# Rectified hidden values by the bank: one rectification per 512 columns instead of two, tiles in pairs, weight roundings in other ticks

## The chip, the cores and the metric

The kernel runs on one core of one Trainium2 chip. The metric is the device time of one execution in microseconds (us), the median of three runs. The engines are named as the profile names them: PE (TensorE, with PEld for its weight loads), DVE (VectorE), ACT (ScalarE), POOL (GpSimd) and SP (SyncE, which issues most DMAs). SBUF is the on-chip memory that all engines reach; PSUM is the memory into which PE writes its products, in banks of 512 fp32 columns.

## What is computed

Attention with global and local keys over 2 x 768 tokens, then a mixture of four experts, then a layer with a softmax-gated unit, a normalisation and an output product. The change touches the experts and, in names alone, the last layer:

```python
x = attention(q, k, v)                      # 1536 x 512
p = domain_probs / domain_probs.sum(-1)
for e in range(4):
    h = np.maximum(x @ w1[e], 0.0)          # 512 -> 1024 hidden values
    out += p[:, e:e + 1] * (h @ w2[e])      # 1024 -> 512
h = out @ w_in;  solu = h * softmax(h)
y = layernorm(solu) * g_ln @ w_out
```

## The kernel before, in words

**Precision.** Every matrix is held as a high part (rounded to PE's fp32r type) and a low part (what the rounding left). A product is three passes on PE: high x high, high weights x low tokens, low weights x high tokens. So for each rectified tile two instructions are needed: ACT writes the high part `fhh` (Relu, which rounds on writing) and DVE writes the low part `fhl`, max(x, 0) minus the high part.

**Order of work.** The experts are cut into eight halves (`he` = 0 to 7) of 512 hidden values. For each half from the second on, the product x @ w1 of tokens 0 to 1023 comes from seven block products instead of eight (`paired_groups`, L639: "paired group" below), once for each of two hidden halves q. From `he` = 2 on the last 512 tokens also come from seven block products (`tail_groups`, L559: "tail group" below), six times in all. The order on PE in one half is: tail group, second product h @ w2 of the last 512 tokens (four output tiles, L524), paired group, second product of tokens 0 to 511, second product of tokens 512 to 1023. The whole program is written out in order by hand (`manual_schedule`): each engine runs its instructions in the order of the code, and waits by semaphores on what it reads or overwrites.

**The tail group** issues the block products in the order 1, 2, 6, 5, 7, 3, 4 (L579), each of 12 matmuls of 256 columns, into three banks: products 1, 6, 7 and 4 into bank a, one after the other, product 2 into b, 5 and 3 into c. ACT copies products 1, 6 and 5 to SBUF (L594). DVE adds (L599): 1 + 2 into b, 5 + 7 into b, 6 + the sum in c into c. Below these are "sum 2", "sum 7" and "sum 3". After each sum, and for product 4 straight from bank a, `hidden` (L571) rectifies the bank's 512 columns in two halves, one for each q:

```python
for q in range(2):
    t = src[:, q_ * q:q_ * q + q_]
    th, tl = (d[2 * q + odd][:, q_ * half:q_ * half + q_] for d in h3)
    nc.scalar.activation(th, t, AF.Relu)                          # L575, ACT
    nc.vector.scalar_tensor_tensor(out=tl, in0=t, ...)            # L576, DVE
```

Hidden tiles 0 and 2 (`odd` = 0) come from products 2 and 3, tiles 1 and 3 (`odd` = 1) from 7 and 4. The first output tile of the second product (`g2`, dt = 0, L524) takes its twelve matmuls in a sorted order: the four high ones of tiles 0 and 2, the four of tiles 1 and 3, then the four low ones.

**The paired group** issues 1, 2, 6, 5, 7, 4, 3, each for q = 0 and then q = 1, with 6 matmuls of 512 columns for each q. There are two banks each of a, b and c. ACT copies products 1, 6 and 7 to SBUF (L673); DVE makes sum 2 in b, sum 7 (the copy of 7 plus bank c) in SBUF over the copy, and sum 3 in c (L677); L654 on ACT and L655 on DVE rectify 512 columns at a time. Product 4 goes to bank a after product 7.

**Weights.** A ring of w2 pieces is loaded by SP (L279, alternately into `kr` and `frawt`), rounded by ACT into `wV` (L295) and completed by POOL (L303). `tick` (L414) starts this: it runs steps that are due, and begins new pieces (`split_steps`, L307) that were loaded at least two ticks ago. `moe` calls `tick` after each group, in the tail group after products 2, 5, 3 and 4 (L781). The same ticks issue the conversion of the last layer's double-precision weights (L186 to L203, most of it on DVE).

**Tiles.** The pool of rectified tiles (L792) has eight buffers of 128 x 512 for each of the tags "hh" and "hl".

## Time and profile before

| | us |
|---|---|
| median of 3 runs (746.58 to 746.95) | 746.9 |
| the profiled execution, whole | 746.98 |
| its span, first to last instruction | 745.2 |
| PE busy | 729.3 |
| DVE, ACT, POOL busy | 476.6, 296.7, 261.4 |

The span is what the trace shows; the profiled execution is 1.8 us longer than its span and 0.1 us longer than the median. A matmul's busy time is modelled and matmuls overlap, so PE's pace is read from start to start, not from the duration of one. In a timeline row the number after "x" is how many like instructions were merged, and a bracket at the end gives the idle time of the engine just before and what ended it.

### The profile page before, as it was taken

The page shows a single profiled execution, that of the slowest core. Times are in us where ns is not written, and L with a number is a line of the kernel's source. Part 1 is how long each engine was busy: PE and PEld are TensorE (multiplying, and loading weights), DVE is VectorE, ACT ScalarE, POOL GpSimd, SP SyncE. Part 2 cuts the span into 40 slices and gives each one's busy share as a digit, 9 for nine tenths or more (in the row PEclk, how much of TensorE's full clock was granted, in tenths as well). Part 3 has the DMA queues.
Part 4 walks back from the last instruction along what each step waited for, and adds up shares of the span by engine and source line. Part 5 has one row for each costly group of instructions (what it writes and reads, how often), then busy time and mean ns, then how long its engine had stood idle before and what let it go on. Part 6 is the DMA issues. An engine that isn't in the chain of part 4 may idle for free.

```text
span 745.2 us, 11046 instructions
## 1 busy us (share of the span) xinstructions
PE 729.3 (98%) x3917; PEld 600.8 (81%) x3917; DVE 476.6 (64%) x1064; ACT 296.7 (40%) x692; POOL 261.4 (35%) x294
## 2 busy tenths in 40 slices
PE   8999999999999999999999999999999999999997
PEld 6687877888887888888788888878888888888886
DVE  6787867647694696668568567765842646655551
ACT  4777766422522333233243424324333323243252
POOL 5600044475783163208306423540644231000000
PEclk9999999999999999999999999999999999999999
DMA  8623421212242132223223222322210820222221
GB/s 248 169 90 108 116 72 44 85 42 72 83 136 79 56 101 70 85 85 114 72 60 96 67 90 85 113 63 66 70 29 29 327 96 9 62 76 75 63 73 48
DMA packets 49985, 65.70 MB, mean 88 GB/s; under 512 B 6656, under 2 KB 31488, under 8 KB 49920
## 3 DMA queue, kind: packets, MB, share of 16 engines
q1 hardware_dynamic: 49360, 64.47, 27.6%
q8 instruction: 33, 0.54, 0.3%
q10 hardware_dynamic: 560, 0.43, 0.2%
q14 instruction: 32, 0.26, 0.1%
HBM read 49.12 MB, written 11.56 MB: 81 GB/s over the span
## 4 chain that ended last, share of the span: by engine, by line
PE 91%; DVE 4%; ACT 4%; issue 1%; DVEq 0%; ACTq 0%
PE fg L524 35%; PE fg L668 18%; PE fo L897 9%; PE fh L836 9%; PE fg L589 6%; PE fg L500 5%; PE x L1095 2%; PE sps L991 2%; PE pt L1073 2%; ACT fhh L575 2%; DVE fg L599 1%; DVE fhl L576 1%; PE wp L132 1%; PE wp L1178 1%; ACT wV L295 1%
## 5 line engine op out<-in xcount | busy, mean ns | idle before, releaser
L524 PE MATMUL fg<-fhh,wV 128*128 128x512 f32 (+1 forms) x800 | 248.2, 387 | 6.6 <-ACT fhh L575 4.4
L524 PEld LDWEIGHTS fg<-fhh,wV 128*128 128x128 f32 x800 | 146.9, 188 | 46.0 <-ACT fhh L575 15.5
L524 PE MATMUL fg<-fhl,wV 128*128 128x512 f32 (+1 forms) x400 | 149.3, 381 | 0.0
L524 PEld LDWEIGHTS fg<-fhl,wV 128*128 128x128 f32 x400 | 75.0, 188 | 14.8 <-DVE fhl L510 0.2
L303 POOL TENSOR_TENSOR wR<-kr,wR 128x512 fp32r<-128x512 f32 (+1 forms) x28 | 29.0, 1060 | 112.0 <-ACT wR L295 112.0
L668 PE MATMUL fg<-xt,fwS 128*128 128x512 f32 x252 | 58.3, 389 | 0.0
L668 PEld LDWEIGHTS fg<-xt,fwS 128*128 128x128 f32 x252 | 47.3, 188 | 9.8
L668 PE MATMUL fg<-xh,wR 128*128 128x512 f32 x168 | 55.0, 394 | 0.0
L532 DVE TENSOR_TENSOR fg<-fg,pb 128x512 f32<-128x512 f32 x60 | 41.5, 692 | 13.4 <-PE fg L524 13.4
L897 PE MATMUL fo<-xt,fth 128*128 128x512 f32 (+1 forms) x156 | 45.4, 375 | 0.0
L537 POOL TENSOR_TENSOR scr<-scr,kr 128x512 f32<-128x512 f32 x24 | 31.0, 1292 | 40.1 <-DVE kr L536 40.1
L1051 ACT ACTIVATE p<-p,mn 128x256 f32<-128x256 f32 x68 | 33.8, 498 | 27.4 <-DVE mn L1046 27.4
L886 POOL TENSOR_SCALAR fva<-fva 128x1 f32<-128x1 f32 x12 | 3.8, 313 | 113.9 <-ACT scr L885 113.9
L533 DVE TENSOR_TENSOR scr<-fg,scr 128x512 f32<-128x512 f32 x60 | 41.5, 692 | 2.0
L655 DVE SCALAR_TENSOR_TENSOR fhl<-fg,fhh 128x512 fp32r<-128x512 f32 x42 | 28.3, 689 | 19.5 <-ACT fhh L654 19.5
L500 PE MATMUL fg<-xh,wR 128*128 128x512 f32 (+1 forms) x128 | 39.5, 373 | 0.0
L654 ACT ACTIVATE fhh<-fg 128x512 fp32r<-128x512 f32 x42 | 24.3, 595 | 38.0 <-DVE fg L677 37.9
L668 PEld LDWEIGHTS fg<-xh,wR 128*128 128x128 f32 x168 | 31.5, 188 | 8.3 <-ACT kr L673 1.9
L673 ACT COPY kr<-fg 128x512 f32<-128x512 f32 x42 | 24.1, 586 | 31.5 <-PE fg L668 31.5
L200 ACT CAST fr<-fcvs 128x256 fp32r<-128x256 f32 x32 | 11.9, 373 | 61.2 <-DVE fcvs L196 50.8
L303 POOL TENSOR_TENSOR fwS<-kr,fwS 128x512 fp32r<-128x512 f32 x28 | 35.7, 1298 | 1.2 <-ACT fwS L295 1.2
L536 DVE TENSOR_TENSOR kr<-fg,pb 128x512 f32<-128x512 f32 x24 | 16.6, 691 | 28.2 <-PE fg L524 24.7
(213 smaller groups left out, 1545.2 us busy)
## 6 DMA issues: line engine op xcount, KB each, us to landing
kr<-in_wall_dram SPq DMA_DIRECT2D x42, 256.0 KB, 2.6
fr<-in_w_dram SPq DMA_DIRECT2D x32, 256.0 KB, 2.7
w_dram<-fr SPq DMA_DIRECT2D x32, 256.0 KB, 2.4
v<-in_vp_dram SPq DMA_DIRECT2D x10, 512.0 KB, 3.5
frawt<-in_wall_dram SPq DMA_DIRECT2D x14, 256.0 KB, 2.7
xt<-w_dram SPq DMA_DIRECT2D x6, 512.0 KB, 10.3
kr<-in_qk_dram SPq DMA_DIRECT2D x22, 128.0 KB, 3.9
out_dram<-scr SPq DMA_DIRECT2D x11, 256.0 KB, 2.2
```

The lines of the kernel that those rows point to most:

```text
L303: e.tensor_tensor(out=w[:, 1], in0=t, in1=w[:, 0].bitcast(F32), op=ALU.subtract)
L500: nc.tensor.matmul(ps[:, :n], lhsT=w[:, a, k], rhs=b[:, k, cols], start=(k == 0 and i == 0), stop=(k == 3 and i == 2))
L524: nc.tensor.matmul(ps[:, :n], lhsT=w[:, a, k], rhs=b[k], start=(i == 0), stop=(i == 11))
L532: nc.vector.tensor_tensor(out=ps[:, :n], in0=ps[:, :n], in1=pb[:, cols], op=ALU.mult)
L533: nc.vector.tensor_tensor(out=a, in0=ps[:, :n], in1=a, op=ALU.add)
L537: nc.gpsimd.tensor_tensor(out=a, in0=a, in1=t, op=ALU.add)
L589: nc.tensor.matmul(ps[:, q_ * q:q_ * q + q_], lhsT=w[:, a, j], rhs=x[b][j], start=(opens and q == j == m == 0), stop=(j == 1 and m == 2), ...
L655: nc.vector.scalar_tensor_tensor(out=tl, in0=src, scalar=0.0, in1=th.bitcast(F32), op0=ALU.max, op1=ALU.subtract)
L668: nc.tensor.matmul(ps, lhsT=w[:, a, j], rhs=x[b][j], start=(i in (1, 2, 5) and j == 0 and m == 0), stop=(j == 1 and m == 2), skip_group_ch ...
L836: nc.tensor.matmul(ps[:, hf], lhsT=a[:, k, cs], rhs=w[:, b], start=(k == 0 and i == 0), stop=(k == 3 and i == 2))
L897: nc.tensor.matmul(ps, lhsT=a[:, fc % 4], rhs=wo[fc][:, b, c0:c0 + n], start=(fc == 0 and i == 0), stop=(fc == 7 and i == 2))
L1051: nc.scalar.activation(p[:, a], p[:, a], AF.Exp, bias=mn[:, a:a + 1], scale=-1.0, accum_out=st_rs[u][:, a, 0:1])
```

## The change

One operation on ACT and one on DVE now rectify a whole bank in the tail group; two tiles of rectified values become the halves of one 128 x 2 x 512 buffer (four of them for each tag), so that a bank's columns for q = 0 and q = 1 lie behind one another and the second product reads its tile as two pieces of 256 columns. In the paired group the copy to SBUF is taken of product 5 instead of 7, and sum 7 is read from bank a and written to bank b. The weight roundings of the tail group are begun only in the tick after product 2, and pieces may be begun one tick after their load there and in the last block of each half.

```diff
--- before.py
+++ after.py
@@ -411,7 +411,7 @@
 
             return [load, nothing, one, both, parts, store]
 
-        def tick(split=True, quiet=False):
+        def tick(split=True, quiet=False, wait=2):
 
             st.now += 1
             for w in st.work:
@@ -424,7 +424,7 @@
                 f()
             if split:
                 for _ in range(2):
-                    w = split_steps(wait=2)
+                    w = split_steps(wait=wait)
                     if w:
                         st.work.append(w)
             load_piece()
@@ -473,12 +473,15 @@
                 yield
             load_pb(0, 0, NT)
 
+        def two_tiles():
+            return [st.hp.tile([128, 2, HALF], F32R, tag=tag, name=f"{arm}{tag}") for tag in ("hh", "hl")]
+
         def gemm_groups(he, blk, last, given=None):
 
 
             c0, n = blk
             cols = slice(c0, c0 + n)
-            hh, hl = [None] * 4, [None] * 4
+            hh, hl, twos = [None] * 4, [None] * 4, []
 
             def g1(ft):
                 if st.pre and he == 0 and c0 == 0:
@@ -501,8 +504,13 @@
                                          start=(k == 0 and i == 0), stop=(k == 3 and i == 2))
                     if k < 3:
                         yield 3 * n / 2.4
-                th = st.hp.tile([128, n], F32R, tag="hh", name=f"{arm}hh")
-                tl = st.hp.tile([128, n], F32R, tag="hl", name=f"{arm}hl")
+                if st.wS is None:
+                    th = st.hp.tile([128, n], F32R, tag="hh", name=f"{arm}hh")
+                    tl = st.hp.tile([128, n], F32R, tag="hl", name=f"{arm}hl")
+                else:
+                    if ft % 2 == 0 or not twos:
+                        twos[:] = two_tiles()
+                    th, tl = (x[:, ft % 2, :n] for x in twos)
                 if ft == 3 and st.wS is None:
                     nc.vector.tensor_scalar(th, ps[:, :n], 0.0, None, op0=ALU.max)
                 else:
@@ -564,17 +572,16 @@
                      for i, k0, cols in ((1, 0, lo), (2, 2, lo), (3, 2, hi), (4, 0, hi))}
             for i, f in ((5, 0), (6, 1), (7, 2)):
                 right[i] = [[st.xt3[f][j][:, b] for j in range(2)] for b in range(2)]
-            for d, tag in zip(h3, ("hh", "hl")):
-                d[:] = [st.hp.tile([128, HALF], F32R, tag=tag, name=f"{arm}{tag}") for _ in range(4)]
+            twos = [two_tiles() for _ in range(2)]
+            for d, w in zip(h3, range(2)):
+                d[:] = [twos[odd][w].rearrange("p h (q c) -> p q h c", q=2)[:, q] for q in range(2) for odd in range(2)]
             banks, kept = {}, {}
 
             def hidden(src, odd, half):
-                for q in range(2):
-                    t = src[:, q_ * q:q_ * q + q_]
-                    th, tl = (d[2 * q + odd][:, q_ * half:q_ * half + q_] for d in h3)
-                    nc.scalar.activation(th, t, AF.Relu)
-                    nc.vector.scalar_tensor_tensor(out=tl, in0=t, scalar=0.0, in1=th.bitcast(F32),
-                                                   op0=ALU.max, op1=ALU.subtract)
+                th, tl = (x[:, half] for x in twos[odd])
+                nc.scalar.activation(th, src, AF.Relu)
+                nc.vector.scalar_tensor_tensor(out=tl, in0=src, scalar=0.0, in1=th.bitcast(F32),
+                                               op0=ALU.max, op1=ALU.subtract)
 
             for i in (1, 2, 6, 5, 7, 3, 4):
                 c = {1: "a", 6: "a", 7: "a", 4: "a", 2: "b", 5: "c", 3: "c"}[i]
@@ -646,11 +653,12 @@
             right = {1: raw_x(0, lo), 2: raw_x(2, lo), 3: raw_x(2, hi), 4: raw_x(0, hi)}
             for i, f in ((5, 0), (6, 1), (7, 2)):
                 right[i] = [[xt[:, f, b, j] for j in range(2)] for b in range(2)]
-            banks, kept = {}, {}
+            banks, kept, twos = {}, {}, []
 
             def hidden(src, dst, ft):
-                th = st.hp.tile([128, HALF], F32R, tag="hh", name=f"{arm}hh")
-                tl = st.hp.tile([128, HALF], F32R, tag="hl", name=f"{arm}hl")
+                if ft < 2:
+                    twos[:] = two_tiles()
+                th, tl = (x[:, ft // 2] for x in twos)
                 nc.scalar.activation(th, src, AF.Relu)
                 nc.vector.scalar_tensor_tensor(out=tl, in0=src, scalar=0.0, in1=th.bitcast(F32),
                                                op0=ALU.max, op1=ALU.subtract)
@@ -668,13 +676,12 @@
                         nc.tensor.matmul(ps, lhsT=w[:, a, j], rhs=x[b][j],
                                          start=(i in (1, 2, 5) and j == 0 and m == 0), stop=(j == 1 and m == 2),
                                          skip_group_check=(i not in (1, 2, 5)))
-                if i in (1, 6, 7):
+                if i in (1, 6, 5):
                     kept[q, i] = sc_b[(2 if i == 6 else 0) + q]
                     nc.scalar.copy(kept[q, i], ps)
                 if i in (2, 7, 3):
-                    s, u = kept[q, {2: 1, 7: 7, 3: 6}[i]], banks[q, "b" if i == 2 else "c"]
-                    t = s if i == 7 else u
-                    nc.vector.tensor_tensor(out=t, in0=s, in1=u, op=ALU.add)
+                    t = banks[q, "c" if i == 3 else "b"]
+                    nc.vector.tensor_tensor(out=t, in0=kept[q, {2: 1, 7: 5, 3: 6}[i]], in1=ps, op=ALU.add)
                     hidden(t, *((h1, 2 * q) if i == 2 else (h2, 2 * q + 1) if i == 7 else (h2, 2 * q)))
                 elif i == 4:
                     hidden(ps, h1, 2 * q + 1)
@@ -753,7 +760,7 @@
                 for cost in g:
                     yield 0, cost
                 st.tick(st.wS is not None, quiet=(he == 0 and gi < 4) or (given is None and gi in (1, 2))
-                        or (last and gi == 3))
+                        or (last and gi == 3), wait=1 if last and he else 2)
             if he % 2 and he < NHE - 1:
                 st.later.append((st.now + 2, he // 2 + 1, blk))
 
@@ -778,7 +785,7 @@
                 for i in st.tail_groups(he, h3):
                     yield 0, 0.0
                     if i in (2, 5, 3, 4):
-                        st.tick(quiet=True)
+                        st.tick(i == 2, True, 1)
                 yield from run(he, (2 * HALF, 512), False, h3)
             h1, h2 = ([[None] * 4, [None] * 4] for _ in range(2))
             for i in st.paired_groups(he, h1, h2):
@@ -789,7 +796,7 @@
 
     def rest_of_moe(st, arm, gen):
         with ExitStack() as es:
-            st.hp = hp = es.enter_context(tc.tile_pool(name=f"{arm}h", bufs=8))
+            st.hp = hp = es.enter_context(tc.tile_pool(name=f"{arm}h", bufs=4))
             st.wS = es.enter_context(tc.tile_pool(name=f"{arm}wS", bufs=1)).tile([128, 4, 2, 512], F32R, name=f"{arm}wS")
             st.cvp = es.enter_context(tc.tile_pool(name=f"{arm}cvp", bufs=2))
             st.rawt = es.enter_context(tc.tile_pool(name=f"{arm}rawt", bufs=1)).tile([128, 512], F32, name=f"{arm}rawt")
@@ -863,9 +870,9 @@
             def tr(t):
                 tt = t_b[t % 2]
                 res = []
+                twos = [hp.tile([128, 2, HALF], F32R, tag=tag, name=f"{arm}t") for tag in ("hh", "hl")]
                 for g in range(2):
-                    th = hp.tile([128, 512], F32R, tag="hh", name=f"{arm}th")
-                    tl = hp.tile([128, 512], F32R, tag="hl", name=f"{arm}tl")
+                    th, tl = (x[:, g] for x in twos)
                     if 1 < t < NSLOT - 2:
 
                         pt = tq_b[t % 2].rearrange("p (i g c q) -> p g i c q", i=4, g=2, c=4)[:, g]
```

The order of instructions on PE, SP and POOL is the same as before but for names and lines. On ACT and DVE it changes in the tail and paired groups. ACT in the first tail group, before (`fg_2569` is bank a, `fg_2583` b, `fg_2614` c):

```order
L575 ACTIVATE fhh_2561<-fg_2583 128x256
L575 ACTIVATE fhh_2563<-fg_2583 128x256
L594 COPY kr_78<-fg_2569 128x512
L594 COPY kr_78<-fg_2614 128x512
L295 CAST wV_67<-kr_78 128x512
L575 ACTIVATE fhh_2562<-fg_2583 128x256
L575 ACTIVATE fhh_2564<-fg_2583 128x256
L575 ACTIVATE fhh_2561<-fg_2614 128x256
L575 ACTIVATE fhh_2563<-fg_2614 128x256
L295 CAST wV_67<-frawt_1826 128x512
L575 ACTIVATE fhh_2562<-fg_2569 128x256
L575 ACTIVATE fhh_2564<-fg_2569 128x256
```

and now (a, b and c are `fg_2549`, `fg_2563`, `fg_2594`):

```order
L582 ACTIVATE fhh_2545<-fg_2563 128x512
L295 CAST wV_67<-kr_78 128x512
L601 COPY kr_78<-fg_2549 128x512
L601 COPY kr_78<-fg_2594 128x512
L295 CAST wV_67<-frawt_1826 128x512
L582 ACTIVATE fhh_2547<-fg_2563 128x512
L582 ACTIVATE fhh_2545<-fg_2594 128x512
L582 ACTIVATE fhh_2547<-fg_2549 128x512
```

Four rectifications stand where eight stood. The rounding from `kr` has moved from behind the copy of product 5 to ahead of the copy of product 6, and the rounding from `frawt` from between the rectifications of products 3 and 4 to ahead of that of product 7.

The end of the second paired group on ACT, before (`fg_2762` and `fg_2770` are the a banks):

```order
L673 COPY kr_78<-fg_2762 128x512
L654 ACTIVATE fhh_2850<-kr_78 128x512
L673 COPY kr_78<-fg_2770 128x512
L654 ACTIVATE fhh_2862<-kr_78 128x512
L654 ACTIVATE fhh_2872<-fg_2762 128x512
L654 ACTIVATE fhh_2882<-fg_2770 128x512
```

and now (`fg_2734` and `fg_2742` are the a banks, `fg_2793` and `fg_2801` the c banks, `fg_2751` and `fg_2763` the b banks):

```order
L681 COPY kr_78<-fg_2793 128x512
L681 COPY kr_78<-fg_2801 128x512
L200 CAST fr64_2713<-fcvs_1830 128x256
L662 ACTIVATE fhh_2821<-fg_2751 128x512
L662 ACTIVATE fhh_2821<-fg_2763 128x512
L662 ACTIVATE fhh_2840<-fg_2734 128x512
L662 ACTIVATE fhh_2840<-fg_2742 128x512
```

The two copies of bank a between the rectifications are gone; two copies of the c banks stand ahead of them. The same place on DVE, before:

```order
L677 TENSOR_TENSOR kr_78<-kr_78,fg_2823 128x512
L655 SCALAR_TENSOR_TENSOR fhl_2851<-kr_78,fhh_2850 128x512
L677 TENSOR_TENSOR kr_78<-kr_78,fg_2830 128x512
L655 SCALAR_TENSOR_TENSOR fhl_2863<-kr_78,fhh_2862 128x512
L655 SCALAR_TENSOR_TENSOR fhl_2873<-fg_2762,fhh_2872 128x512
L655 SCALAR_TENSOR_TENSOR fhl_2883<-fg_2770,fhh_2882 128x512
```

and now:

```order
L684 TENSOR_TENSOR fg_2751<-kr_78,fg_2734 128x512
L663 SCALAR_TENSOR_TENSOR fhl_2822<-fg_2751,fhh_2821 128x512
L684 TENSOR_TENSOR fg_2763<-kr_78,fg_2742 128x512
L663 SCALAR_TENSOR_TENSOR fhl_2822<-fg_2763,fhh_2821 128x512
L663 SCALAR_TENSOR_TENSOR fhl_2841<-fg_2734,fhh_2840 128x512
L663 SCALAR_TENSOR_TENSOR fhl_2841<-fg_2742,fhh_2840 128x512
```

The two sums now read the a banks themselves and write the b banks, in the same order with the low parts: the second sum still stands behind the first low part.

## Rows read from the trace of the kernel before

**Rows 1.** The page, parts 1 and 4: busy time by engine; the chain that ended last
```profile
PE 729.3 (98%) x3917; PEld 600.8 (81%) x3917; DVE 476.6 (64%) x1064; ACT 296.7 (40%) x692; POOL 261.4 (35%) x294
...
PE 91%; DVE 4%; ACT 4%; issue 1%; DVEq 0%; ACTq 0%
```

**Rows 2.** Waits by engine and line, PE: us in total, times, longest us
```profile
PE fg L524 <- ACT fhh L575: 4.4, 6, 0.7
```

**Rows 3.** The chain in order of time, 220 to 420 us: start us, us, what
```profile
220.59 7.25 PE fg L589 x60
...
227.91 0.71 DVE fg L599
...
230.28 0.70 DVE fg L599
...
231.00 0.39 ACT fhh L575
...
232.26 0.51 ACT wV L295
...
263.01 21.76 PE fg L524 x96
...
356.25 0.71 DVE fg L599
```

**Rows 4.** Timeline of the first tail group, 218 to 236 us: start us, us, engine line op
```profile
226.43 0.59 ACT L594 COPY kr<-fg 128x512 f32<-128x512 f32 x1 [0.37 <-PE fg L589]
...
230.42 0.28 PE L589 MATMUL fg<-xh,wR 128*128 128x256 f32 x1
...
231.44 3.27 PE L524 MATMUL fg<-fhh,wV 128*128 128x512 f32 x8 [0.74 <-ACT fhh L575]
...
235.47 0.39 PE L524 MATMUL fg<-fhh,wV 128*128 128x512 f32 x1
```

**Rows 5.** Timeline of the second paired group, all engines, 247 to 261 us
```profile
247.98 0.70 DVE L677 TENSOR_TENSOR fg<-kr,fg 128x512 f32<-128x512 f32 x1 [1.26 <-PE fg L668]
...
248.71 0.60 ACT L654 ACTIVATE fhh<-fg 128x512 fp32r<-128x512 f32 x1 [1.47 <-DVE fg L677]
...
249.34 0.69 DVE L655 SCALAR_TENSOR_TENSOR fhl<-fg,fhh 128x512 fp32r<-128x512 f32 x1 [0.66 <-ACT fhh L654]
249.95 0.69 DVE L677 TENSOR_TENSOR fg<-kr,fg 128x512 f32<-128x512 f32 x1
...
256.13 0.59 ACT L673 COPY kr<-fg 128x512 f32<-128x512 f32 x1 [0.58 <-PE fg L668]
...
258.01 0.57 ACT L673 COPY kr<-fg 128x512 f32<-128x512 f32 x1
...
258.63 0.19 PEld L668 LDWEIGHTS fg<-xh,wR 128*128 128x128 f32 x1 [0.30 <-ACT kr L673]
```

**Rows 6.** Line L668's instructions: what its engine waited for (us, times)
```profile
  ACT kr L673: 1.9, 7
```

**Rows 7.** Line L655's instructions: durations ns min/median/max, first and last start
```profile
L655 DVE SCALAR_TENSOR_TENSOR fhl<-fg,fhh x42: 678/692/694, 185.4 to 585.9; 128x512 fp32r<-128x512 f32 x42
L655 DVE SCALAR_TENSOR_TENSOR fhl<-kr,fhh x14: 691/693/1117, 194.0 to 580.8; 128x512 fp32r<-128x512 f32 x14
```

**Rows 8.** Timeline of SP's queue, 200 to 560 us: the loads of L279
```profile
221.51 0.33 SPq L279 DMA_DIRECT2D frawt<-in_wall_dram  x1
...
350.85 0.33 SPq L279 DMA_DIRECT2D frawt<-in_wall_dram  x1
```

**Rows 9.** Line L279's instructions: their DMAs' time to landing
```profile
DMA to landing us min/median/max: 2.5/2.7/3.3
```

**Rows 10.** Timeline of another paired group, 447 to 449.6 us
```profile
447.11 0.42 DVE L198 TENSOR_TENSOR fr<-fr,fcvs 128x256 f32<-128x256 f32 x1
...
448.52 0.59 ACT L673 COPY kr<-fg 128x512 f32<-128x512 f32 x1
```

**Rows 11.** The page, part 6: DMA issues, KB each, us to landing
```profile
xt<-w_dram SPq DMA_DIRECT2D x6, 512.0 KB, 10.3
```

## The prediction

> **What bounds the kernel now.** The page comes first: PE is busy for 729.3 of 745.2 us, and the chain that ended last runs over PE for 91% and over DVE and ACT for 4% each [rows 1]. So PE sets the time wherever it has something to do, and a change that leaves its matmuls as they are can gain only where the chain leaves PE. The waits of PE name one such place in the expert stage: six waits on line L575, the rectification in the tail group [rows 2]. The chain in order of time shows what stands there. At 227.91 us it leaves PE for sum 7 on DVE, and then runs through rectifications, low parts, sum 3 and a weight rounding, ACT and DVE in turn, until PE takes over [rows 3]. It does so once in each of the six tail groups.
>
> The timeline of the first tail group shows what the place costs [rows 4]. The last matmul of product 4 starts at 230.42, and such matmuls follow each other at 7.25 / 60 = 0.12 us [rows 3], so PE could go on at 230.54. The second product starts at 231.44, its first eight matmuls are spread over 3.27 us where they need some 1.8, and the next output tile starts at 235.47. Twelve matmuls at the undisturbed pace of 21.76 / 96 = 0.2267 us [rows 3] take 2.72 us. So 235.47 - 230.54 - 2.72 = 2.21 us are lost in a tail group, 13.3 us in six: that is the ceiling of what the change can gain there.
>
> The paired groups hold the other wait, a small one: PE waits seven times, 1.9 us in all, for the ACT copy of product 7, since product 4 goes into the same bank [rows 6]; in the trace the weight load at 258.63 is the one that was held [rows 5].
>
> **Tail group: one rectification for a bank, and the rounding out of its way.** The durations of whole-bank operations, and what one leaves between itself and the next, are taken from the same work in the paired group, where 512 columns are handled at a time already [rows 5]: from the start of a sum to the start of its rectification 248.71 - 247.98 = 0.73 us, from there to the low part 0.63, from a low part to the next sum on DVE 0.61; a rectification takes 0.60.
>
> Sum 7 starts at 227.91 as before, since PE's order ahead of it is unchanged. Then its rectification starts at 228.64, its low part at 229.27, and sum 3 at 229.88 (before: 230.28 [rows 3]); product 3 is long done (its last matmul is 12 x 0.12 us ahead of that of product 4, at 228.98). The rectification of sum 3 starts at 230.61 and ends at 231.21. Before, the first half of it started at 231.00 and ended at 231.39 [rows 3], and PE followed 0.05 us later [rows 4]; so PE starts at 231.26, only 0.18 us earlier. What changes is what follows. The rectification of product 4 no longer has the rounding of 0.51 us ahead of it [rows 3] nor a low part between its halves: it starts behind that of sum 3, at 231.21 at the latest, ends at 231.81, and PE wants it four matmuls on, at 231.26 + 0.91 = 232.17. The low part of 3 starts at 231.24, that of 4 at 231.85, and the latter ends at 232.54; PE wants the low ones after eight matmuls, at 233.07. So none of the twelve is late any more, and the next output tile starts at 231.26 + 2.72 = 233.98 instead of 235.47: 1.49 us in a tail group, **8.9 us in six**. Of the 2.21 us lost, 0.72 stay: the start, which the chain sum 7, rectify, low part, sum 3, rectify still sets. That chain is what is late next.
>
> The two roundings that move: the one from `kr` now stands ahead of the copy of product 6, which frees bank a for product 7; but ahead of both there is now one rectification of 0.60 us instead of two of 0.39 with a low part between them, and the difference covers the rounding's 0.51, so I cost it at nothing. The one from `frawt` fills the time in which ACT waits for sum 7; its load was issued at 221.51 [rows 8] and lands 2.7 us later [rows 9], at 224.2, while ACT reaches it after the copy of product 5, at 226.43 + 0.59 = 227.02 [rows 4]: 2.8 us of cover. POOL's low parts and the next loads follow earlier than before.
>
> **Paired group: sum 7 reads the bank.** Before, ACT's copy freed the second bank a at 258.01 + 0.57 = 258.58, and PE's load followed at 258.63 [rows 5]. Now DVE frees it, with its second sum 7, which stands on DVE behind the first sum, the first rectification (ACT) and the first low part. The first sum can start when the first copy did, at 256.13; then 0.73 + 0.63 + 0.61 us to the second sum and 0.69 us for it, which is 258.79, and PE at 258.84. That is 0.21 us later, in each of seven paired groups: **1.5 us lost**. Its bounds are nil (if the 0.05 us of slack and the shorter read of PSUM make it up) and one operation of DVE more, as below. The copies of product 5 that replace those of 7 run while PE still has both products 7 to do. What waits behind the longer wait: all of PE, in order; rectifications and low parts of the group are not due until the second product, over 2 us later.
>
> The low part now reads a bank where it read SBUF: the rows show 692 ns from a bank and 693 from SBUF [rows 7], so this costs nothing. The Trainium skill (VectorE: DVE Perf Modes, the section on the TRN2 errata) gives a DVE instruction 58 fixed cycles from SBUF and 120 from PSUM, which at its 0.96 GHz would make each low part 0.065 us longer and the seven groups 0.5 us dearer, an estimate from that page. This trace does not agree with it, and the sum goes by the rows.
>
> **Reading tiles in two pieces.** The second product of the tail group now reads its tiles as two pieces of 256 columns. The trace has no such read at full width. From below it costs nothing; from above, each of the 288 matmuls (12 x 4 output tiles x 6) costs what two matmuls of 256 columns do, 2 x 0.1208 instead of 0.2267 us [rows 3], 4.3 us in all. I take nothing, because the columns streamed are the same in number and the extra in that row is per instruction, of which there is still one.
>
> The pairing of tiles itself removes no work and adds no wait that I can place: a buffer's former values were read before the tail group began. The last layer has the same order and sizes.
>
> **Sum.** 8.9 - 1.5 = 7.4 us off the profiled execution's 746.98 us: 739.6; the median stands 0.1 lower, so **739.5 us**. The saving reaches the end, because PE has no other wait in the expert stage that could take it back.
>
> **Rivals.** *Two pieces are slow:* the pace of PE's second product in the tail falls as bounded above, 739.5 + 4.3 = 743.8. Against it: nothing in the rows shows a matmul that pays by piece; for it: nothing excludes it. 7%.
>
> *DVE is not free for sum 7.* Before, the copy on ACT shielded PE from DVE; now a conversion operation (0.42 us) that DVE still has ahead of the first sum 7 holds PE. In the tightest group the last one ends at 447.53, and PE's signal comes at 448.52, 0.99 us later [rows 10]. If the conversions slip so that one operation too many stands there in each group, 7 x 0.42 = 2.9 us are lost, 742.4; 5%. With three, 8.8 us are lost and the change comes to nothing, 748.3 at worst; together with the case that two tiles in a buffer make ACT wait for the other half's readers and nothing is gained at all (746.9), 5%.
>
> *The moved rounding blocks ACT (slower).* In the tail group ACT now takes the rounding from `frawt` before the rectification of sum 7. If the load has not landed, everything behind it waits: rectifications 7, 3 and 4, and PE with them. ACT is due at sum 7 at 228.64 and the rounding holds it 0.51 us, so a load that lands after 228.13, 6.6 us after its issue, delays the chain one for one, and beyond 6.6 + 1.5 = 8.1 us the tail group is slower than before. At 10.3 us, which 512 KB loads take elsewhere [rows 11], it is 3.7 - 1.5 = 2.2 us worse, six times, and with the paired groups 746.9 + 13.2 + 1.5 = 761.6. Against it: these loads landed in 3.3 us at most [rows 9], and the one issued latest in its tail group, at 350.85 [rows 8] for a sum 7 at 356.25 [rows 3], 1.0 us later in it than the first, keeps 1.2 us of cover even then. 4%.
>
> **How the numbers follow.** The forecast as worked out has 79%. The range goes from 737.5 (nothing lost in the paired groups, and 0.5 us more gained by waits too small for the sum) to 743.8 (two pieces at their upper bound), which takes in one conversion in the way. A measurement of this kernel can tell about 0.2%, 1.5 us, from no change: faster by more than that are the forecast and the first two rivals, 79 + 7 + 5 = 91%; within it 5%; slower 4%.
>
> **What would show it.** Right: PE's waits on the tail rectification shrink to one short one per tail group, the next output tile starts 6.1 us after sum 7 instead of 7.6, no rounding stands between rectifications, and PE's held weight load in the paired group grows by some 0.2 us and names DVE. Wrong: ACT waiting for a DMA in the tail group, second-product matmuls there more than 0.23 us apart with no wait, or conversions on DVE between product 7 and its sum.

## The result: 6.6 us faster, in the tail groups

The changed kernel takes 740.1 us (median of 4 runs, 739.95 to 740.36); the kernel before took 746.7 beside it (746.57 to 746.95). The ratio is 0.9911, with an interval of 0.9894 to 0.9929. The forecast was 739.5. The profiled execution took 740.11 us, with a span of 738.2 where it was 745.2.

The page of the changed kernel, parts 1 and 4 (before: [rows 1]):

```profile
PE 725.0 (98%) x3917; PEld 601.8 (82%) x3917; DVE 473.0 (64%) x1040; ACT 293.2 (40%) x668; POOL 260.7 (35%) x294
...
PE 85%; DVE 5%; ACT 4%; issue 3%; POOL 2%; DMA 0%; DVEq 0%; ACTq 0%; POOLq 0%
```

PE has the same 3917 instructions; DVE and ACT have 24 fewer each, which are the 24 second halves of six tail groups. The chain's shares are of little use here: ahead of the tail groups, from some 158 to 194 us, it now runs over POOL and a piece of 10.16 us of "issue" where it ran over PE before, though PE is busy throughout in both. The waits tell more. First the waits of PE's weight loads before, then those after (us in total, times, longest us):

```profile
PEld fg L524 <- ACT fhh L575: 15.5, 24, 0.9
...
PEld fg L668 <- ACT kr L673: 1.9, 7, 0.3
```

```profile
PEld fg L532 <- ACT fhh L582: 4.5, 6, 0.8
PEld fg L676 <- DVE fg L684: 3.6, 7, 0.5
```

Four waits in each tail group have become one, and in the paired groups DVE holds PE for longer than ACT did. The first tail group after (start us, us, engine line op; the rows to compare are [rows 4]):

```profile
227.81 0.70 DVE L606 TENSOR_TENSOR fg<-kr,fg 128x512 f32<-128x512 f32 x1 [2.23 <-PE fg L596]
229.17 0.69 DVE L583 SCALAR_TENSOR_TENSOR fhl<-fg,fhh 128x512 fp32r<-128x512 f32 x1 [0.66 <-ACT fhh L582]
229.78 0.69 DVE L606 TENSOR_TENSOR fg<-kr,fg 128x512 f32<-128x512 f32 x1
...
230.50 1.09 ACT L582 ACTIVATE fhh<-fg 128x512 fp32r<-128x512 f32 x2 [1.36 <-DVE fg L606]
231.12 1.29 DVE L583 SCALAR_TENSOR_TENSOR fhl<-fg,fhh 128x512 fp32r<-128x512 f32 x2 [0.66 <-ACT fhh L582]
...
231.15 2.14 PE L532 MATMUL fg<-fhh,wV 128*128 128x512 f32 x8 [0.56 <-ACT fhh L582]
...
234.04 0.39 PE L532 MATMUL fg<-fhh,wV 128*128 128x512 f32 x1
```

From sum 7 to the next output tile it is 234.04 - 227.81 = 6.23 us; it was 235.47 - 227.91 = 7.56 [rows 3, 4]. Six times 1.33 us are 8.0; in the other five groups it is 6.21 to 6.23 us, and was 7.55 to 7.56. The second paired group, DVE and the load it holds (compare [rows 5]):

```profile
254.71 0.70 DVE L684 TENSOR_TENSOR fg<-kr,fg 128x512 f32<-128x512 f32 x1 [1.05 <-PE fg L676]
256.07 0.69 DVE L663 SCALAR_TENSOR_TENSOR fhl<-fg,fhh 128x512 fp32r<-128x512 f32 x1 [0.66 <-ACT fhh L662]
256.68 0.69 DVE L684 TENSOR_TENSOR fg<-kr,fg 128x512 f32<-128x512 f32 x1
...
257.42 0.19 PEld L676 LDWEIGHTS fg<-xh,wR 128*128 128x128 f32 x1 [0.52 <-DVE fg L684]
...
257.75 0.39 PE L676 MATMUL fg<-xl,wR 128*128 128x512 f32 x1
```

The load is held for 0.52 us instead of 0.30. Seven times 0.22 is 1.5 us, so 8.0 - 1.5 = 6.5 of the 6.6 us are placed.

### The profile page after: what moved, and what is told of

Its sections match the earlier page's. It is cut to its first block, busy times and chain, and to the rows that moved or that the text cites. A ratio compares the mean times of both kernels' runs of the same rounds, so it can differ in the third digit from the quotient of the medians.

```text
span 738.2 us, 11012 instructions
## 1 busy us (share of the span) xinstructions
PE 725.0 (98%) x3917; PEld 601.8 (82%) x3917; DVE 473.0 (64%) x1040; ACT 293.2 (40%) x668; POOL 260.7 (35%) x294
## 4 chain that ended last, share of the span: by engine, by line
PE 85%; DVE 5%; ACT 4%; issue 3%; POOL 2%; DMA 0%; DVEq 0%; ACTq 0%; POOLq 0%
PE fg L532 35%; PE fg L676 14%; PE fo L904 9%; PE fh L843 9%; PE fg L596 6%; PE fg L503 4%; PE x L1102 2%; PE sps L998 2%; PE pt L1080 2%; DVE fg L684 1%; DVE fg L606 1%; ACT fhh L582 1%; PE wp L1185 1%; ACT fhh L662 1%; DVE fhl L663 1%
## 5 line engine op out<-in xcount | busy, mean ns | idle before, releaser
L532 PE MATMUL fg<-fhh,wV 128*128 128x512 f32 (+1 forms) x800 | 243.5, 384 | 3.4 <-ACT fhh L582 3.3
L663 DVE SCALAR_TENSOR_TENSOR fhl<-fg,fhh 128x512 fp32r<-128x512 f32 x56 | 38.1, 690 | 31.8 <-ACT fhh L662 31.8
L662 ACT ACTIVATE fhh<-fg 128x512 fp32r<-128x512 f32 x56 | 32.7, 598 | 58.9 <-DVE fg L684 55.1
L904 PE MATMUL fo<-xt,ft 128*128 128x512 f32 (+1 forms) x234 | 51.8, 374 | 0.0
L904 PEld LDWEIGHTS fo<-xt,ft 128*128 128x128 f32 x234 | 41.5, 188 | 7.6
L684 DVE TENSOR_TENSOR fg<-kr,fg 128x512 f32<-128x512 f32 x42 | 28.9, 689 | 21.6 <-PE fg L676 18.8
```

The source lines that it names most:

```text
L532: nc.tensor.matmul(ps[:, :n], lhsT=w[:, a, k], rhs=b[k], start=(i == 0), stop=(i == 11))
L662: nc.scalar.activation(th, src, AF.Relu)
L663: nc.vector.scalar_tensor_tensor(out=tl, in0=src, scalar=0.0, in1=th.bitcast(F32), op0=ALU.max, op1=ALU.subtract)
L684: nc.vector.tensor_tensor(out=t, in0=kept[q, {2: 1, 7: 5, 3: 6}[i]], in1=ps, op=ALU.add)
L904: nc.tensor.matmul(ps, lhsT=a[:, fc % 4], rhs=wo[fc][:, b, c0:c0 + n], start=(fc == 0 and i == 0), stop=(fc == 7 and i == 2))
```

## Experiments

Ten kernels. Each edit is made in the changed kernel, but for one that is made in the kernel before. "Changed" is 740.11 us throughout; the kernel before took 746.55 to 746.75 beside the various runs.

### The paired group's copy of 7 again

```diff
-                if i in (1, 6, 5):
+                if i in (1, 6, 7):
...
-                    t = banks[q, "c" if i == 3 else "b"]
-                    nc.vector.tensor_tensor(out=t, in0=kept[q, {2: 1, 7: 5, 3: 6}[i]], in1=ps, op=ALU.add)
+                    s, u = kept[q, {2: 1, 7: 7, 3: 6}[i]], banks[q, "b" if i == 2 else "c"]
+                    t = s if i == 7 else u
+                    nc.vector.tensor_tensor(out=t, in0=s, in1=u, op=ALU.add)
```

> The changed kernel with the paired group's old order: product 7 is copied by ACT and sum 7 lies over the copy; everything else as in the change. Theory (the wait for DVE's second sum 7 costs PE 0.21 us in each of seven paired groups): 740.1 - 7 x 0.21 = 738.6 us, PE's held weight load is released by ACT again and its seven waits fall from 3.6 us to about 1.9. Rival A (the longer hold is made up elsewhere, so the paired change costs nothing): 740.1. Rival B (sums and low parts out of PSUM are worth more than the hold, so the old order is dearer): 741 or more.

Measured: 738.72 us (738.43 to 738.81), 1.39 below the changed kernel, as the theory said. The waits of its weight loads:

```profile
PEld fg L532 <- ACT fhh L582: 4.5, 6, 0.8
...
PEld fg L676 <- ACT kr L681: 1.9, 7, 0.3
```

The tail's row is that of the changed kernel, and the paired group's is that of before. So this part of the change costs 1.4 us, for the reason given.

### The old ticks

```diff
-                        st.tick(i == 2, True, 1)
+                        st.tick(quiet=True)
...
-                        or (last and gi == 3), wait=1 if last and he else 2)
+                        or (last and gi == 3))
```

> The changed kernel with the ticks of before: the rounding from frawt stands between the rectifications of products 3 and 4 again; whole-bank rectifications stay. Theory (most of the gain comes from whole banks, the rounding's place matters by what the rectification of 4 is then late): the rectification of 3 starts at 230.50, the rounding 0.50 later, that of 4 ends near 232.1, PE's fifth weight load would be due near 231.95, so 0.15 to 0.25 us in each of six tail groups: 741.0 to 741.6 us. Rival (the gain is the rounding's move): 0.5 us or more in each, 743 to 747. Rival (no one waits for it): 740.1.

Measured: 740.66 us (740.38 to 740.85), 0.55 above the changed kernel. That is less than the theory's 0.9 to 1.5, and it excludes the rival by which the roundings' move is the gain. The rows of the first tail group show a second hold, before the fifth load:

```profile
230.93 0.76 PEld L532 LDWEIGHTS fg<-fhh,wV 128*128 128x128 f32 x4 [0.76 <-ACT fhh L582]
231.94 0.76 PEld L532 LDWEIGHTS fg<-fhh,wV 128*128 128x128 f32 x4 [0.25 <-ACT fhh L582]
```

Its idle time is 0.25 us, but the next output tile comes only 0.05 us later than in the changed kernel: from sum 3 (229.56) it starts after 4.31 us (233.87) where the changed kernel has 4.26. Six times 0.05 is 0.3; the other 0.25 of the 0.55 is placed nowhere, and is less than the spread of either kernel's runs.

### Halves again, roundings moved

```diff
-                th, tl = (x[:, half] for x in twos[odd])
-                nc.scalar.activation(th, src, AF.Relu)
-                nc.vector.scalar_tensor_tensor(out=tl, in0=src, scalar=0.0, in1=th.bitcast(F32),
-                                               op0=ALU.max, op1=ALU.subtract)
+                for q in range(2):
+                    t = src[:, q_ * q:q_ * q + q_]
+                    th, tl = (x[:, half, q_ * q:q_ * q + q_] for x in twos[odd])
+                    nc.scalar.activation(th, t, AF.Relu)
+                    nc.vector.scalar_tensor_tensor(out=tl, in0=t, scalar=0.0, in1=th.bitcast(F32),
+                                                   op0=ALU.max, op1=ALU.subtract)
```

> The changed kernel with the tail group's rectification in two halves of 256 columns again, into the same paired buffers; the roundings stay moved. Theory (whole banks bring most): the rows of before with the rounding's 0.40 taken out give 7.56 - 0.40 = 7.16 us from sum 7 to the next output tile, where the changed kernel has 6.23, so 0.93 in each of six: 740.1 + 5.6 = 745.7 us. Rival (the roundings' move brings most): 741 to 742. This run and the one with the old ticks together tell whether the two gains add: if they do, what they lose sums to about 6 x 1.33 = 8.0.

Measured: 749.15 us (748.76 to 749.55), ratio to before 1.0036 (1.0023 to 1.0048): slower than the kernel before, and 3.4 us above what I expected. The expected 0.93 us in the second product is there (228.19 to 235.28, 7.09 us for 7.16). What I had not seen stands earlier in the group, on ACT and then on PE:

```profile
224.09 0.38 ACT L584 ACTIVATE fhh<-fg 128x256 fp32r<-128x256 f32 x1 [1.63 <-DVE fg L608]
224.97 0.38 ACT L584 ACTIVATE fhh<-fg 128x256 fp32r<-128x256 f32 x1 [0.49 <-DVE fhl L585]
225.25 0.61 ACT L295 CAST wV<-kr 128x512 fp32r<-128x512 f32 x1
225.76 1.08 ACT L603 COPY kr<-fg 128x512 f32<-128x512 f32 x2
...
226.40 1.69 PE L598 MATMUL fg<-wR,fwS 128*128 128x256 f32 x12 [0.30 <-ACT kr L603]
```

The second half waits 0.49 us for DVE, the rounding from `kr` stands behind it, the copy of product 6 behind that, and PE waits for this copy in each of six groups. Sum 7 starts 228.19 - 220.19 = 8.00 us after the group's first matmul instead of 227.81 - 220.36 = 7.45. So a tail group is 0.55 + 0.86 = 1.41 us longer than with whole banks, 8.5 in six; measured are 9.0. Of the rest, 0.35 stands in the fourth group, where sum 7 starts 8.35 us after the first matmul. The prediction cost the rounding ahead of the copy at nothing because one rectification stands before it instead of two with a low part between them; this run shows the bill where that cover is missing.

### Halves and the old ticks

Both edits above at once.

> The changed kernel with rectification in halves and the ticks of before, both at once: what is left of the change is the paired tiles and the paired group's copy of 5. Theory (the pairs cost nothing, the paired group costs 1.4): 746.55 + 1.4 = 748.0 us. With the halves and the moved roundings the time was 749.15, so the move by itself then costs 1.1 us where banks are rectified in halves, though it gains 0.5 where they are rectified whole; the trace of that run shows the reason that this would confirm: PE waited 6 x 0.3 us for the copy of product 6, which stands behind the rounding from kr. With the old ticks that wait is absent. Rival (halves written into paired tiles cost something by themselves): 749 or more, with or without the old ticks. Rival (the two gains add): 749.15 + 0.55 = 749.7.

Measured: 748.90 us (748.73 to 750.81; two of the five executions took 750.8, the profiled one among them). That lies between theory (748.0) and rival (749 or more), and it does not say that the roundings' move costs 1.1 us in this form: 748.90 against 749.15 is nothing that I would call a difference. PE's wait for the copy of 6 is absent, as expected, but the rounding is back between the rectifications, and the two about balance. Of the 0.9 us over the theory, 0.40 are an idle time before sum 7 in the fourth tail group, which the chain calls "issue" (at 421.64 here; the run with moved roundings has it too, so the faster executions of this kernel may as well, which no trace shows). The rest stays open, and with it the rival that halves cost something in paired tiles by themselves; the next two runs speak against it, for halves in another order.

### The same halves, both rectifications first

```diff
+                qs = [slice(q_ * q, q_ * q + q_) for q in range(2)]
                 th, tl = (x[:, half] for x in twos[odd])
-                nc.scalar.activation(th, src, AF.Relu)
-                nc.vector.scalar_tensor_tensor(out=tl, in0=src, scalar=0.0, in1=th.bitcast(F32),
-                                               op0=ALU.max, op1=ALU.subtract)
+                for q in qs:
+                    nc.scalar.activation(th[:, q], src[:, q], AF.Relu)
+                for q in qs:
+                    nc.vector.scalar_tensor_tensor(out=tl[:, q], in0=src[:, q], scalar=0.0, in1=th[:, q].bitcast(F32),
+                                                   op0=ALU.max, op1=ALU.subtract)
```

> The changed kernel with halves of 256 columns again, as in the run at 749.15, but in another order: ACT takes both halves of a bank, then DVE both low parts. The instructions are the same in number and size as in that run. Theory (halves are dear because ACT and DVE take turns on one bank, each half waiting 0.49 us for the other engine, and hardly because there are two instructions): two rectifications back to back take 0.66 us where one of 512 columns takes 0.60, two low parts 0.76 where one takes 0.69, sum 3 comes 0.1 us later than with whole banks: 740 to 741.5 us. Rival (it is the number of instructions): 747 to 749.

Measured: 739.38 us (739.14 to 739.39): 9.8 us below the same instructions in turns, and 0.7 below the changed kernel. Its first tail group:

```profile
228.25 0.66 ACT L584 ACTIVATE fhh<-fg 128x256 fp32r<-128x256 f32 x2 [1.07 <-DVE fg L609]
...
228.94 0.76 DVE L586 SCALAR_TENSOR_TENSOR fhl<-fg,fhh 128x256 fp32r<-128x256 f32 x2 [0.72 <-ACT fhh L584]
229.61 0.69 DVE L609 TENSOR_TENSOR fg<-kr,fg 128x512 f32<-128x512 f32 x1
...
230.33 1.21 ACT L584 ACTIVATE fhh<-fg 128x256 fp32r<-128x256 f32 x4 [1.42 <-DVE fg L609]
...
230.77 2.12 PE L532 MATMUL fg<-fhh,wV 128*128 128x512 f32 x8 [0.47 <-ACT fhh L584]
```

Two halves back to back take ACT 0.66 us where one whole bank takes 0.60. PE starts 230.77 - 230.33 = 0.44 us after the last sum's first rectification, where it was 0.65 with whole banks: its first load needs the first half only. It is the turns that were dear, and not the number of instructions.

### The kernel before with this order alone

The edit is in the tail group's `hidden` of the kernel before, and is its only one:

```diff
-                for q in range(2):
-                    t = src[:, q_ * q:q_ * q + q_]
-                    th, tl = (d[2 * q + odd][:, q_ * half:q_ * half + q_] for d in h3)
+                ops = [[src[:, q_ * q:q_ * q + q_]] + [d[2 * q + odd][:, q_ * half:q_ * half + q_] for d in h3]
+                       for q in range(2)]
+                for t, th, tl in ops:
                     nc.scalar.activation(th, t, AF.Relu)
+                for t, th, tl in ops:
                     nc.vector.scalar_tensor_tensor(out=tl, in0=t, scalar=0.0, in1=th.bitcast(F32),
                                                    op0=ALU.max, op1=ALU.subtract)
```

> The kernel before with nothing changed but this order in the tail group: both rectifications of a bank, then both low parts. No paired tiles, the old ticks, the copy of 7. Theory (the change's gain is the end of the turns between ACT and DVE on one bank, and the paired tiles only the way to it): the changed kernel's 740.1, less 1.4 for the paired group's copy of 5, more 0.55 for the rounding's old place and up to 0.7 for the halves: 739.2 to 740.0 us. Rival (whole banks in one buffer are needed): 745 to 746.7.

Measured: 738.61 us (738.3 to 738.9), ratio to before 0.9891 (0.9875 to 0.9908). The theory's mechanism was right; the time is 0.6 below its range. ACT's two halves now follow each other at once, in the first tail group for sum 7 and sum 3:

```profile
228.29 0.66 ACT L575 ACTIVATE fhh<-fg 128x256 fp32r<-128x256 f32 x2 [1.07 <-DVE fg L600]
230.37 0.66 ACT L575 ACTIVATE fhh<-fg 128x256 fp32r<-128x256 f32 x2 [1.43 <-DVE fg L600]
```

Two lines in another order gain 8.1 us, more than the whole change. Paired tiles and whole banks were one way to end the turns, and not the better one. This kernel and the one before it both rectify in ordered halves, in separate and in paired tiles; they differ by 0.77 us, where the copy of 5 and the roundings account for 1.39 - 0.55 = 0.84. So in this order pairing the tiles costs nothing that the runs can show.

### Sum 3 ahead of the low part of 7

In the tail group `hidden` puts its low part on a list; the list is emptied after every sum or rectification but that of product 7.

```diff
-                nc.vector.scalar_tensor_tensor(out=tl, in0=src, scalar=0.0, in1=th.bitcast(F32),
-                                               op0=ALU.max, op1=ALU.subtract)
+                lows.append(lambda: nc.vector.scalar_tensor_tensor(
+                    out=tl, in0=src, scalar=0.0, in1=th.bitcast(F32), op0=ALU.max, op1=ALU.subtract))
...
+                while lows and i != 7:
+                    lows.pop(0)()
```

> The changed kernel with one DVE instruction moved in the tail group: the low part of product 7 stands behind sum 3 instead of ahead of it. Theory (the chain sum 7, rectify, low part, sum 3, rectify sets the second product's start): sum 3 then starts when product 3 is done, some 0.38 us behind its last matmul, at 229.25 instead of 229.78, PE starts near 230.62 instead of 231.15, and six tail groups gain 6 x 0.53 = 3.2: 736.9 us. If PE's hold also no longer empties its weight loads, some 0.1 more in each, 736.3. Rival (ACT's rectification of 4 or the later low parts then hold PE, so the gain is given back): 739 to 740. Rival (product 3 is the bound already): 740.1.

Measured: 737.18 us (737.05 to 737.42), 2.9 below the changed kernel for 3.2 expected. PE's load is held for 0.25 us instead of 0.76, and the next output tile starts 5.68 us after sum 7 (228.00 to 233.68) instead of 6.23:

```profile
229.45 0.70 DVE L608 TENSOR_TENSOR fg<-kr,fg 128x512 f32<-128x512 f32 x1 [0.76 <-PE fg L598]
230.06 2.08 DVE L585 SCALAR_TENSOR_TENSOR fhl<-fg,fhh 128x512 fp32r<-128x512 f32 x3
...
230.83 1.68 PEld L532 LDWEIGHTS fg<-fhh,wV 128*128 128x128 f32 x8 [0.25 <-ACT fhh L584]
```

Sum 3 now waits for PE, not for DVE's low part. This confirms what the prediction left standing as "the start, which the chain still sets".

### The second sum 7 ahead of the first low part

The same list in the paired group, kept over the first of the two sums 7:

```diff
+                while lows and (i, q) != (7, 0):
+                    lows.pop(0)()
```

> The changed kernel with one DVE instruction moved in the paired group: the second sum 7 stands ahead of the first low part of product 7 instead of behind it; the copies stay those of product 5. Theory (the hold of bank a comes from the low part that stands ahead of the second sum): the second sum starts when PE has finished product 7, near 256.07 instead of 256.68, and ends 0.61 earlier than PE's load wants it or nearly so; the whole delay of the matmul behind the held load, 257.75 - (255.80 + 7 x 0.227) = 0.36 us, goes, in seven groups 2.5: 740.1 - 2.5 = 737.6 us, below the 738.7 of the copy of 7. If only the 0.21 is won back: 738.6. Rival (the wait is for the bank's own readout, so the order on DVE changes nothing): 740.1. Rival (first low parts come late for the second product of tokens 0 to 511): 740 or more.

Measured: 737.12 us (736.95 to 737.48), 3.0 below the changed kernel where 2.5 were worked out (the other 0.5 stays open), and 1.6 below the copy of 7. The second sum starts at 256.08 (256.68 in the changed kernel), the waits of PE's loads have no row for this place any more, and the load that was held follows the one before it after 0.22 us (257.18 to 257.40). So reading the bank was not a bad idea; the order on DVE was what made it cost something.

### Both orders, and both with halves

The two edits together:

> The changed kernel with both DVE orders: sum 3 ahead of the low part of 7 in the tail group, and the second sum 7 ahead of the first low part in the paired group. Theory (two holds that do not touch each other): the tail order gained 740.1 - 737.2 = 2.9, the paired order is expected to gain 1.5 to 2.5, together 734.7 to 735.8 us. Rival (they share DVE's time, so one gives part of the other back): 736.5 or more.

Measured: 734.16 us (734.1 to 734.29). The gains add, as the theory said: 2.93 + 2.99 = 5.92, measured 5.95. To this kernel, one edit more in the tail's `hidden`:

```diff
-                nc.scalar.activation(th, src, AF.Relu)
+                for q in (slice(0, q_), slice(q_, 2 * q_)):
+                    nc.scalar.activation(th[:, q], src[:, q], AF.Relu)
```

> The kernel at 734.16 (both DVE orders) with the tail group's rectification on ACT in two halves back to back, and one low part of 512 columns on DVE behind both. Theory (PE's first loads of the second product need only the first half of the last sum's bank, which is rectified some 0.2 us earlier): PE's hold, 0.25 us in the trace of that kernel, falls to about 0.05 in each of six tail groups, and no rectification gets in the way, since two halves take 0.66 us where one takes 0.60: 734.2 - 6 x 0.2 = 733.0 us. Rival (the hold is not the bound any more, since product 3 or the rectification of product 4 is late next): 733.7 to 734.2. Rival (one instruction more on ACT delays the rectification of product 4, which PE wants 0.9 us after the first): 734.5 or more.

Measured: 732.81 us (732.64 to 733.31), ratio to before 0.9817 (0.9804 to 0.9831). The theory holds: no weight load waits for a rectification in the tail any more. From its page and its first tail group:

```profile
PE 96%; DVE 2%; ACT 1%; DMA 0%; issue 0%; DVEq 0%; ACTq 0%
```

```profile
227.32 0.70 DVE L609 TENSOR_TENSOR fg<-kr,fg 128x512 f32<-128x512 f32 x1 [2.16 <-PE fg L599]
...
229.94 1.69 PEld L532 LDWEIGHTS fg<-fhh,wV 128*128 128x128 f32 x8
...
232.82 0.39 PE L532 MATMUL fg<-fhh,wV 128*128 128x512 f32 x1
```

The next output tile starts 5.50 us after sum 7. PE's last matmul of product 4 starts at 229.83 and the second product at 229.95, 0.12 us on, so PE's matmuls keep their pace there. The load starts only 0.01 us ahead of its matmul, though, and by the prediction's own working 232.82 - 229.95 - 2.72 = 0.15 us of the 2.21 are still lost. This is the fastest version found: 13.8 us below the kernel before, 7.3 below the changed one.

## Why the prediction held, and where it was off

**The place and the price of the tail group: right, the size 0.16 us too high.** Sum 7 to the start of the second product was to take 231.26 - 227.91 = 3.35 us and takes 3.34. The next output tile was to follow 2.72 us after that and follows after 2.89, so the term of 8.9 us was 8.0. The step that failed is "starts at 231.26 + 2.72": it gave the twelve matmuls the undisturbed pace from the recorded start of the first one. In undisturbed work a load runs ahead of its matmul; here the first load was held until 231.14, and its matmul's record starts at 231.15:

```profile
231.14 1.70 PEld L532 LDWEIGHTS fg<-fhh,wV 128*128 128x128 f32 x8 [0.76 <-ACT fhh L582]
...
233.82 0.19 PEld L532 LDWEIGHTS fg<-fhh,wV 128*128 128x128 f32 x1
```

The loads keep the pace from there (the thirteenth starts at 233.82, 2.68 us on), and the thirteenth matmul 0.22 us behind its load. After a hold, then, the lead has to be paid for once. The Trainium skill (TensorE: Matmul & The Clock Gate, section "Step-by-step: what each phase is for") says that PE pulls weight loads ahead of running matmuls; the rows agree as to the lead of 0.22 us and show what its loss costs.

**What makes the gain: named only in part.** The prediction put it on "one rectification for a bank, and the rounding out of its way". The roundings' new places are some 0.55 us of it, as undoing them showed. The rest is that ACT and DVE no longer take turns on one bank. ACT in the kernel before, in the first tail group:

```profile
231.00 0.38 ACT L575 ACTIVATE fhh<-fg 128x256 fp32r<-128x256 f32 x1 [1.09 <-DVE fg L599]
231.87 0.38 ACT L575 ACTIVATE fhh<-fg 128x256 fp32r<-128x256 f32 x1 [0.49 <-DVE fhl L576]
232.15 0.61 ACT L295 CAST wV<-frawt 128x512 fp32r<-128x512 f32 x1
232.66 0.39 ACT L575 ACTIVATE fhh<-fg 128x256 fp32r<-128x256 f32 x1
233.54 0.38 ACT L575 ACTIVATE fhh<-fg 128x256 fp32r<-128x256 f32 x1 [0.49 <-DVE fhl L576]
```

Each second half waits 0.49 us for the first half's low part, though it reads other columns and writes another tile; what they share is the bank. The Trainium skill (PSUM — Partial Sum Buffer, section "PSUM bank collisions raise a hardware error") says that two engines may not be at one bank at once, reads included, and that the compiler back end puts a dependency between any two such instructions of different engines. The rows agree: the wait stands between two reads of different columns, and is gone where DVE's turn comes after both of ACT's. On different banks the two overlap: in the changed kernel DVE starts the low part of product 3 (bank c) at 231.12, while ACT's second rectification (bank a) ends at 230.50 + 1.09 = 231.59. The prediction saw the low part between the halves and did not ask whether its order could be changed without touching sizes. The terms, as the runs measure them, close: 8.1 (the order alone) - 0.7 (whole banks instead of ordered halves) + 0.55 (the roundings) - 1.4 (the copy of 5) = 6.6 us, and 6.6 were measured.

**The roundings cost nothing where they went: right.** ACT in the first tail group after:

```profile
224.26 0.60 ACT L582 ACTIVATE fhh<-fg 128x512 fp32r<-128x512 f32 x1 [1.63 <-DVE fg L606]
224.76 0.61 ACT L295 CAST wV<-kr 128x512 fp32r<-128x512 f32 x1
225.26 0.59 ACT L601 COPY kr<-fg 128x512 f32<-128x512 f32 x1
...
226.85 0.62 ACT L295 CAST wV<-frawt 128x512 fp32r<-128x512 f32 x1
228.54 0.60 ACT L582 ACTIVATE fhh<-fg 128x512 fp32r<-128x512 f32 x1 [1.07 <-DVE fg L606]
```

The copy of product 6 starts 1.73 us after sum 2 (223.53 to 225.26), where it was 1.88 (223.60 to 225.48), and the rectification of sum 7 waits 1.07 us for DVE, not for a load. The rival of a late load did not come true.

**The paired group: right.** 1.5 us were forecast, and undoing this part gave 1.39. The hold grew from 0.30 to 0.52 us, as the chain through DVE said. No conversion stood in the way: the last one before the first sum ends on DVE at 253.66, and the sum starts at 254.71 behind PE. That the low part reads a bank costs nothing: in the kernel with the copy of 7, which has both forms, the medians are 692 ns from a bank and 693 from SBUF.

**Tiles in two pieces: right at nothing.** In the changed kernel the next output tile starts at 234.04 and the paired group behind it at

```profile
242.20 0.39 PE L676 MATMUL fg<-xh,wR 128*128 128x512 f32 x1
```

so 36 matmuls on such tiles take 8.16 us, 0.2267 each, the undisturbed pace; before, from 235.47 to 243.63, they took the same.

**What to see, seen otherwise:** PE's own waits on the rectification were said to become one per tail group; there were six already before [rows 2], and they only shrank from 4.4 to 3.3 us. The loads' waits, 24 before and 6 after, were the ones to name.

## What to carry to other kernels

Where two engines work on one PSUM bank in pieces, try all of the first engine's pieces ahead of the second's: the turns cost 8 us here, and the order of two lines was worth more than larger operations and paired buffers. When a wait moves from an engine with one instruction there to one with a queue, look at what stands ahead in that queue and whether it is needed sooner. After PE has been held, count its pace from the held weight load and add the load's lead.

## What the runs showed of the hardware

PE's clock fell behind such holds once. In the run with halves and the old ticks the profiled execution took 750.81 us, 1.9 above the median. Its fourth tail group held PE's first load for 1.28 us, and then three times more for some 0.5. The first matmuls behind that hold, and then the busy time by stretch (us, PE, PEld, DVE, ACT, POOL, then the granted clock, DMA share and GB/s):

```profile
425.56 3.77 PE L532 MATMUL fg<-fhh,wV 128*128 128x512 f32 x8 [1.07 <-ACT fhh L584]
```

```profile
423.00:427.00 4.00, 2.79 (x17) 1.87 (x15) 2.30 (x5) 1.92 (x6) 0.04 (x1) 1.00 0.27 66
427.00:431.00 4.00, 3.94 (x10) 2.65 (x10) 0.85 (x2) 0.56 (x2) 1.24 (x1) 0.57 0.41 126
431.00:435.00 4.00, 4.00 (x20) 3.25 (x19) 2.90 (x6) 0.86 (x2) 1.64 (x2) 1.00 0.03 9
```

Behind a stretch of 4 us in which PE was busy for 2.79, the granted clock was 0.57 over the next 4. By quarter microseconds it reads 0.99 from 427.25 to 427.50 and then 0.50, the lower of its two levels (1.2 GHz), until 430.75; by 431 it is at 1.00 again. The four low-part matmuls took 1.91 us there, where they take 1.08 in the changed kernel's first group. PE was never idle for more than 1.07 us at a time before the fall, and the fourth of the held loads came only after it. The Trainium skill (TensorE: Matmul & The Clock Gate, section "What's actually happening") puts the lower level on an idle engine; the rows show it behind an engine that had paused once for 1.07 us and then more briefly. Why it fell here stays open, for the run with halves and moved roundings has the same pause in its fourth tail group, and PE busy for the same 2.79 us from 423 to 427, and its clock reads 1.00 there and over the next 4 us:

```profile
425.44 2.81 PE L532 MATMUL fg<-fhh,wV 128*128 128x512 f32 x8 [1.07 <-ACT fhh L584]
```

In the other eleven profiles no stretch of 4 us from 20 to 728 us has a granted clock below 0.97, so in these no fall of the clock came on top of what PE's holds cost by their own length and the load's lead.
